# Block 0's loads issued from two engines, masks in a tile of their own, strided heads' rows of block 0 contiguous

## The chip, the cores and the metric

One core of a Trainium2 chip runs the whole program. The metric is the device time of one execution in microseconds (us); of several runs the median counts. The engines are TensorE (PE, with its weight loads as PEld), VectorE (DVE), ScalarE (ACT), GpSimd (POOL) and SyncE (SP), which here only issues DMAs. Sixteen DMA engines move the data.

## The reference

Attention over 4 batches, 8 heads, 576 positions and 64 columns per head feeds two gated feed-forward layers, all in float32 (the weights come as 64-bit words that the kernel converts):

```python
scores = scale * np.matmul(q, k.transpose(0, 1, 3, 2))
mask_local = (rel >= 0) & (rel < stride)                       # heads 0 to 3, stride 32
mask_strided = (rel >= 0) & (pos[None, :] % stride == pos[:, None] % stride)   # heads 4 to 7
attn = softmax(np.where(masks, scores, -1e9)); x = np.matmul(attn, v)
xn = x / rms(x) * rms_g;  h = silu(xn @ w_gate) * (xn @ w_val);  y = h @ w_out   # 2304 x 512, 1536
a = y @ w_a;  b = y @ w_b;  out = (a * b) @ w_out2
```

## The kernel before

The 576 positions are cut into six blocks of 96; a block of all four batches is 384 columns. Every float32 operand of a large product is split into a high and a low part, and three matmuls (L481, L482, L483) make one product.

For each block t, `attention(t, ...)` (L187) makes a dictionary of steps. Local heads go through TensorE: `load_local` (L201) loads queries and keys, `qk` the scores of three groups of units (L296), `smask` the mask and scale on VectorE (L314), `lmax`, `lexp` (one ACTIVATE per unit, L336, or one for the group, L333), `lnorm`, `pt` (transposes with the identity, L358), `ptc`, `pv` (L378). Strided heads never touch TensorE for their scores: `load_q` (L225) and `load_kv` (L232) load rows by residue, `sqk` multiplies on GpSimd (L248) and sums on VectorE (L251), `ssub`, `sexp` (L264), `snorm` (L273) make the softmax, `spv` (L281, L284) the weighted sum, `xst` the transposes. `pvc` and `xstc` write the block's activations `xx` (L387, L389) and their squares (L432); `rinv` (L448, L450) is the inverse root mean square.

No block runs ahead of block 0. Its loads are issued first, in the order of a string, and its steps in the order of another:

```python
LOADS0 = "la0 lq ls0 cst la1 lb0 lvl1 lb1 lvl0 lv0"
```

All of these are issued by SyncE: `la0` and `la1` are queries (L207, its first 512 columns) and keys (L208) of the two halves of local heads, `lb0`, `lb1` the other 256 columns of queries (L213), `lq`, `ls0`, `lv0` the strided heads' queries (L227), keys and values (L236), `lvl0`, `lvl1` the local heads' values (L219). `cst` (L569) is one tile of 388 columns with the identity (128), two masks (192 and 64) and the norm weights (4); `ident`, `mask_a`, `mask_b`, `g_sb` are views of it. Strided rows lie in HBM as 18 rows per head, and block t takes some of them per head (`qs[:, :, 3*t:3*t+3, :]` and `src[:, heads(g), :L, :]`), so a partition's share of block 0 is four pieces of 768 bytes.

Behind them SyncE issues the weights of 12 units (`load_units(NFC)`, L572 and L111), 24 transfers of 512 KB. Each is turned into float32r parts by `convert1` and `conversion`: on ACT L137, L142 and L150, on VectorE L145, on GpSimd L151. Then 12 chunks `fc` of the hidden layer run for each block (L740): `g_ps` and `v_ps` (24 matmuls), the gate, and `emit_y` of the chunk before (12 groups of matmuls). While block 0 runs, the remaining weights are converted and block 1's attention is computed.

Before qk0 TensorE runs 20 idle matmuls (`keep_busy(WARM)`, L563), and 36 more behind `pv` and the transposes (`id36`).

The order of instructions on an engine is not the written one: `TileContext(nc, schedule_with_timeline_sim=True)` (L1040) plans it when the program is built, by its own estimate of when each operand is there. `tc.issue_after(i)` keeps the instructions of a block behind i on i's engine; `gate(fc)` (L582) uses it, and so does `sqrt_set` (L423), which brings the table of the square root in early by one small activation.

Of the kernel before, what the change touches and what calls it, by code (L numbers as in the profile page):

```python
# [10 lines left out]
F32 = mybir.dt.float32  # L11
# [7 lines left out]
B, H, S, D = 4, 8, 576, 64  # L19
DM, FF, NT = 512, 1536, 2304  # L20
W = 32
PB = 96
NB = S // PB
NTB = B * PB
NM = S // W
NFC = FF // 128
NCC = DM // 128
# [8 lines left out]

LOADS0 = "la0 lq ls0 cst la1 lb0 lvl1 lb1 lvl0 lv0"
STEPS0 = ("sqk00 sqk01 sqk02 qk0 qk1 qk2 smask0 lmax0 lexp0 smask1 lmax1 lexp1 smask2 ssub sexp "  # L40
          "lnorm0 snorm lmax2 lexp2 pt0 ptc0 lnorm1 sqrt_set pt1 ptc1 spv00 spv01 spv02 lnorm2 pt2 "
          "ptc2 pv0 pvc0 pv1 pvc1 xst0 xst1 xstc0 id36 xstc1 rms rinv")
# [29 lines left out]
NEG = -1000000000.0  # L72
BIG = 3.0e38
# [1 line left out]


@with_exitstack
def fused_kernel(ctx: ExitStack, tc: tile.TileContext, qtl, ktl, vl, qs, ks, vs, cst, w1, w2, out):

# [2 lines left out]
    nc = tc.nc  # L84
# [102 lines left out]
    def attention(t, pool, psum, banks):  # L187

        L = 3 * (t + 1)
        G = {0: 4, 1: 2}.get(t, 1)  # L190
        KX, KB = (12 * D, 2) if t < 2 else (NM * D, 3)
        st = {}
        steps = {}

        def bank():
            return psum.tile([128, 512], F32, tag=next(banks), name="att")
# [4 lines left out]
        def load_local(hf, first=False):  # L201

            def f():
                q_t = st["q", hf] = pool.tile([128, 8 * PB], F32, tag="q", name="q_t", bufs=2)
                k_t = st["k", hf] = pool.tile([128, 4, 128], F32, tag="k", name="k_t", bufs=2)
                n = 512 if first else 8 * PB
                nc.sync.dma_start(q_t[:, :n], qtl[t, hf, :, :n])  # L207
                nc.sync.dma_start(k_t, ktl[t, hf])  # L208
            return f

        def load_rest(hf):
            def f():
                nc.sync.dma_start(st["q", hf][:, 512:], qtl[t, hf, :, 512:])  # L213
            return f

        def load_vlocal(hf):
# [5 lines left out]
        def heads(g):  # L222
            return slice(g * G, g * G + G)

        def load_q():  # L225
            q_t = pool.tile([128, 4, 3, D], F32, tag="qx", name="qs_t", bufs=1)
            nc.sync.dma_start(q_t, qs[:, :, 3 * t:3 * t + 3, :])  # L227
            st["qs"] = q_t
            st["S"] = pool.tile([128, 4, 3, 6 if t < 2 else NM], F32, tag="S", name="S_t", bufs=1)
            nc.vector.memset(st["S"], NEG)  # L230

        def load_kv(src, key, g):  # L232
            def f():
                k_t = pool.tile([128, KX], F32, tag="kv", name="kv_t", bufs=KB)
                k_t = k_t[:, :G * L * D].rearrange("p (g n d) -> p g n d", g=G, d=D)
                nc.sync.dma_start(k_t, src[:, heads(g), :L, :])  # L236
                st[key, g] = k_t
            return f

# [182 lines left out]

        def sqrt_set():  # L423

            with tc.issue_after(st["exp"].ins):
                nc.scalar.activation(scr, eps_sb, AF.Sqrt)

        def sq(i):
# [84 lines left out]
    psum = one.enter_context(tc.tile_pool(name="psum", bufs=1, space=bass.MemoryType.PSUM))  # L513
    cpool = ExitStack()
    const1 = cpool.enter_context(tc.tile_pool(name="const1", bufs=1))
    cst_sb = const1.tile([128, 388], F32, name="cst_sb")
    ident = cst_sb[:, 0:128]
    mask_a = cst_sb[:, 128:320].rearrange("p (a k) -> p a k", a=2)
    mask_b = cst_sb[:64, 320:384].rearrange("p (a k) -> p a k", a=1)
    g_sb = cst_sb[:, 384:388]  # L520
    pts = [const1.tile([128, 4, 2, PB], F32, name=f"pt{hf}") for hf in range(2)]
    ones = const1.tile([128, 128], F32, name="ones")
    apool = ExitStack()
# [42 lines left out]
    for p_t in pts:  # L566
        nc.gpsimd.memset(p_t, 0.0)
    s0 = attention(0, pool, psum, itertools.cycle(["att", "y0", "y1", "y2", "y3"]))
    s0["cst"] = lambda: nc.sync.dma_start(cst_sb, cst)  # L569
    for n in LOADS0.split():  # L570
        s0[n]()
    load_units(NFC)  # L572
# [156 lines left out]
    for t in range(NB):  # L729
# [3 lines left out]
        if t == NB - 1:  # L733
            apool.close()
            cpool.close()
            pool = p2.enter_context(tc.tile_pool(name="forms", bufs=1, reuse_waits="tile"))
            early = [f for k in (4, 5, 0, 1, 2, 3) for f in convert_forms(k, k < 4)]
        nxt = attention(t + 1, pool, psum, itertools.cycle(["att"])) if t + 1 < NB else None
        x = [xt[t, cc] for cc in range(NCC)]
        for fc in range(NFC):  # L740
# [206 lines left out]
    for i, (ps, g, p) in enumerate(steps):  # L947
# [12 lines left out]
        a, pa = products(g, 2 * p)  # L960
# [17 lines left out]
def _windows(a):  # L978

    z = np.concatenate([np.zeros(a.shape[:2] + (W, D), a.dtype), a], axis=2)  # L980
    return np.stack([z[:, :, PB * t:PB * t + 128] for t in range(NB)])


def _layout(inputs):
    q, k, v = (np.asarray(inputs[n]) for n in "qkv")
    c = np.ascontiguousarray
    r = {}


    ql = q[:, :4].reshape(2, 2, 2, 2, NB, PB, D).transpose(4, 0, 3, 6, 2, 1, 5)  # L990
    qa = np.zeros((NB, 2, 2, D, 2, 2, 2, 64), q.dtype)
    qb = np.zeros((NB, 2, 2, D, 2, 2, 2, 32), q.dtype)
    for hh in range(2):
        qa[:, :, hh, ..., hh, :] = ql[:, :, hh, ..., :64]
        qb[:, :, hh, ..., hh, :] = ql[:, :, hh, ..., 64:]
    r["qtl"] = np.concatenate([qa.reshape(NB, 2, 128, 512), qb.reshape(NB, 2, 128, 256)], axis=3)
    kw = _windows(k[:, :4]).reshape(NB, 2, 2, 2, 2, 128, D)
    r["ktl"] = c(kw.transpose(0, 1, 4, 6, 3, 2, 5).reshape(NB, 2, 128, 4, 128))
    vw = _windows(v[:, :4]).reshape(NB, 2, 2, 4, 128, D)
    r["vl"] = c(vw.transpose(0, 1, 4, 2, 3, 5))  # L1000

    def st(a):
        return a[:, 4:].reshape(B, 4, NM, W, D)
    r["qs"] = c(st(q).transpose(0, 3, 1, 2, 4).reshape(128, 4, NM, D))
    r["ks"] = c(st(k).transpose(0, 3, 1, 2, 4).reshape(128, 4, NM, D))
    r["vs"] = c(st(v).transpose(0, 3, 1, 2, 4).reshape(128, 4, NM, D))

    def ok(rows, n):
        i, j = np.arange(rows)[:, None] % (rows // 2), np.arange(n)[None, :]
        return (j > i) & (j <= i + W), j  # L1010
    cst = np.zeros((128, 388), np.float32)
    cst[:, 0:128] = np.eye(128)
    m, j = ok(128, 96)
    cst[:, 128:224] = np.where(m & (j >= W), BIG, NEG)
    cst[:, 224:320] = np.where(m, BIG, NEG)
    cst[:64, 320:384] = np.where(ok(64, 64)[0], BIG, NEG)
    cst[:, 384:] = np.asarray(inputs["moe_rms_g"]).reshape(NCC, 128).T
    r["cst"] = cst

    def weights(a, b, o):  # L1020

        a, b, o = (np.asarray(z) for z in (a, b, o))
        a, b = (z.reshape(NCC, 128, NFC, 128).transpose(2, 1, 0, 3).reshape(NFC, 128, DM) for z in (a, b))
        return c(np.stack([a, b, o.reshape(NFC, 128, DM)], axis=1)).view(np.uint64)
    r["w1"] = weights(inputs["moe_w_gate"], inputs["moe_w_val"], inputs["moe_w_out"])
    r["w2"] = weights(inputs["moe2_w_a"], inputs["moe2_w_b"], inputs["moe2_w_out"])
    return r
# [17 lines left out]
```

## Time and profile before

| | us |
|---|---|
| median of 3 runs | 964.13 |
| lowest, highest | 962.64, 965.04 |
| the profiled execution, device time | 965.19 |
| its span, first to last instruction | 963.4 |
| PE busy in the span | 936.9 |
| ACT, DVE, POOL busy | 421.7, 624.8, 541.8 |

A row of a timeline gives the start, the duration, engine, line, operation, tile written <- tiles read, shape, count, and in brackets the idle time of the engine just before it and who ended it. A row of windows gives, for a stretch, busy time (and instructions) of each engine, the granted TensorE clock (1.00 is the full 2.4 GHz, 0.50 is 1.2 GHz), the share of the DMA engines that was busy (packets counted from start to end, so it can pass 1) and the rate.

### The profile page before, as it was taken

How to read it: one execution, taken by the hardware profiler on the slowest of the kernel's cores; microseconds unless marked ns; L12 is line 12 of the kernel's file. 1: busy time of each engine (PE TensorE's matmuls, PEld its weight loads, DVE VectorE, ACT ScalarE, POOL GpSimd, SP SyncE). 2: the span in 40 equal slices, each digit the busy share in tenths (PEclk: the TensorE clock that was granted, in tenths of full speed). 3: DMA queues.
4: the chain of work that ended last, by engine and by line, in shares of the span. 5: the costliest groups of instructions: out<-in, count | busy, mean ns of one | idle time of the engine just before them, and what ended most of it. 6: DMA issues, size and time to landing. Idle time of an engine off the chain costs nothing.

```text
span 963.4 us, 14134 instructions
## 1 busy us (share of the span) xinstructions
PE 936.9 (97%) x5324; PEld 889.0 (92%) x5324; DVE 624.8 (65%) x913; ACT 421.7 (44%) x792; POOL 541.8 (56%) x407
## 2 busy tenths in 40 slices
PE   5998999999999999999999999999999999999998
PEld 4798999999999999999999898999999999999997
DVE  5669867548818895987566378667655655464534
ACT  5987655334433433444555455435425422122110
POOL 3568946458749687969379545654734424123211
PEclk6899999999999999999999999999999999999999
DMA  9964375426534553532788975997993973753701
GB/s 344 408 258 157 110 281 195 159 99 215 175 105 149 174 179 111 177 129 66 270 332 307 358 267 202 369 422 278 359 383 118 341 295 131 290 235 147 259 31 66
DMA packets 57507, 215.55 MB, mean 224 GB/s; under 512 B 5984, under 2 KB 14816, under 8 KB 51808
## 3 DMA queue, kind: packets, MB, share of 16 engines
q1 hardware_dynamic: 57296, 214.53, 61.0%
q8 instruction: 42, 0.69, 0.3%
q14 instruction: 25, 0.20, 0.1%
q10 hardware_dynamic: 144, 0.13, 0.0%
HBM read 172.17 MB, written 42.47 MB: 223 GB/s over the span
## 4 chain that ended last, share of the span: by engine, by line
PE 65%; DVE 7%; POOL 6%; DMA 5%; ACT 4%; issue 4%; SPq 0%; DVEq 0%; ACTq 0%; POOLq 0%
PE o L925 5%; PE o L923 5%; PE o L924 5%; POOL prod L248 4%; DMA raw<-in_w 4%; PE Y L856 4%; PE Y L855 4%; PE Y L854 4%; PE y L482 3%; PE Z L856 3%; PE Z L855 3%; PE Z L854 3%; PE y L483 3%; PE X L854 3%; PE X L856 2%
## 5 line engine op out<-in xcount | busy, mean ns | idle before, releaser
L151 POOL TENSOR_TENSOR hl<-c,hl 128x384 fp32r<-128x384 f32 x72 | 77.4, 1076 | 180.2 <-ACT hl L150 173.6
L248 POOL TENSOR_TENSOR prod<-kv_t,qs_t 128x512 f32<-128x512 f32 (+12 forms) x57 | 107.3, 1903 | 21.5 <-DMA wo<-wod 9.7
L482 PE MATMUL y<-hl,wo 128*128 128x384 f32 x288 | 98.3, 345 | 4.8 <-DVE hl L507 3.7
L281 POOL TENSOR_TENSOR prod<-kv_t,S_t 128x512 f32<-128x512 f32 (+12 forms) x57 | 86.8, 1536 | 22.5 <-issue 8.2
L481 PE MATMUL v_ps<-xx,gv 128*128 128x384 f32 x288 | 97.2, 337 | 1.9 <-DVE sg L760 1.9
L481 PE MATMUL g_ps<-xx,gv 128*128 128x384 f32 x288 | 97.6, 339 | 0.6 <-DVE sg L764 0.6
L482 PE MATMUL v_ps<-xx,gv 128*128 128x384 f32 x288 | 97.6, 339 | 0.0
L483 PE MATMUL v_ps<-xx,gv 128*128 128x384 f32 x288 | 97.2, 338 | 0.0
L483 PE MATMUL g_ps<-xx,gv 128*128 128x384 f32 x288 | 97.1, 337 | 0.0
L482 PE MATMUL g_ps<-xx,gv 128*128 128x384 f32 x288 | 96.8, 337 | 0.0
L861 DVE TENSOR_TENSOR c<-c,Y 128x384 f32<-128x384 f32 x108 | 58.9, 550 | 58.0 <-PE Y L856 53.6
L483 PE MATMUL y<-hl,wo 128*128 128x384 f32 x288 | 95.4, 340 | 0.0
L507 POOL TENSOR_TENSOR hl<-h,hl 128x384 fp32r<-128x384 f32 x60 | 64.9, 1081 | 51.1 <-ACT hl L506 51.0
L284 DVE TENSOR_REDUCE xs_t<-prod 128x64 f32<-128x448 f32 (+17 forms) x57 | 85.9, 1521 | 10.5 <-POOL prod L281 9.4
L481 PE MATMUL y<-hl,wo 128*128 128x384 f32 x288 | 83.7, 342 | 3.7 <-ACT hl L506 2.1
L924 PE MATMUL o<-slab,hl 128*128 128x512 f32 x214 | 83.7, 392 | 0.0
L923 PE MATMUL o<-slab,hl 128*128 128x512 f32 x214 | 83.7, 392 | 0.0
L925 PE MATMUL o<-slab,hl 128*128 128x512 f32 x214 | 82.5, 394 | 0.0
L150 ACT CAST hl<-c 128x384 fp32r<-128x384 f32 x72 | 37.0, 514 | 94.9 <-DVE c L891 94.6
L856 PE MATMUL Y<-slab,form 128*128 128x384 f32 x216 | 73.1, 338 | 0.0
L855 PE MATMUL Y<-slab,form 128*128 128x384 f32 x216 | 73.0, 338 | 0.0
L854 PE MATMUL Y<-slab,form 128*128 128x384 f32 x216 | 73.0, 338 | 0.0
(148 smaller groups left out, 2463.5 us busy)
## 6 DMA issues: line engine op xcount, KB each, us to landing
form<-formd SPq DMA_DIRECT2D x32, 1792.0 KB, 10.6
wo<-wod SPq DMA_DIRECT2D x60, 512.0 KB, 4.1
raw<-in_w SPq DMA_DIRECT2D x40, 512.0 KB, 7.2
gv_raw<-in_w SPq DMA_DIRECT2D x32, 512.0 KB, 10.1
formd<-form SPq DMA_DIRECT2D x6, 1792.0 KB, 7.5
formd<-forms SPq DMA_DIRECT2D x6, 1792.0 KB, 12.5
slab<-x2d SPq DMA_DIRECT2D x24, 384.0 KB, 4.0
wod<-wo SPq DMA_DIRECT2D x12, 512.0 KB, 3.2
```

Source lines behind the costliest of these rows:

```text
L248: nc.gpsimd.tensor_tensor(pr, st["ks", g][:, :, :n, :], st["qs"][:, heads(g), mm:mm + 1, :].to_broadcast([128, G, n, D]), op=ALU.mult)
L281: st["pvm"] = nc.gpsimd.tensor_tensor(pr, st["vs", g][:, :, :n, :], st["S"][:, heads(g), mm, :n, None].to_broadcast([128, G, n, D]), op=AL ...
L284: st["pvr"] = nc.vector.tensor_reduce(st["xs"][:, mm, heads(g), :], pr.rearrange("p g n d -> p g d n"), axis=X, op=ALU.add)
L481: nc.tensor.matmul(out_ps, w_hi, x_hi, start=start, stop=False)
L482: nc.tensor.matmul(out_ps, w_hi, x_lo, start=False, stop=False)
L483: nc.tensor.matmul(out_ps, w_lo, x_hi, start=False, stop=stop)
L854: nc.tensor.matmul(bank(n), hi, x[p][:, 0, c], start=begins and c == 0, stop=False, skip_group_check=not begins)
L855: nc.tensor.matmul(bank(n), hi, x[p][:, 1, c], start=False, stop=False, skip_group_check=not begins)
L856: nc.tensor.matmul(bank(n), lo, x[p][:, 0, c], start=False, stop=c == 1, skip_group_check=not begins)
L923: nc.tensor.matmul(o, h[:, 0, cols], w[0], start=n == 0, stop=False)
L924: nc.tensor.matmul(o, h[:, 0, cols], w[1], start=False, stop=False)
L925: nc.tensor.matmul(o, h[:, 1, cols], w[0], start=False, stop=n == len(chunks) - 1)
```

## The change

Block 0's loads are divided between SyncE and ScalarE's queue (`second` is ScalarE for t = 0 and SyncE otherwise): ScalarE issues both key loads, the masks, the strided keys, `lb1` and the identity, six in all; SyncE issues the other seven. The order is now masks second, `lb1` and `cst` ahead of the local values. The tile `cst` becomes two: `masks` (masks and norm weights, 260 columns) and `cst` (the identity, 128 columns). The strided queries are laid out by block for every t, and block 0 gets copies `ks0` and `vs0` of its keys and values, so that a partition's share is one piece of 3072 bytes. `sqrt_set` is also held behind `sexp`. `s0["w0"]` is defined but named in neither order string. A load's bytes stay the same, but for the tile that is cut in two.

```diff
-LOADS0 = "la0 lq ls0 cst la1 lb0 lvl1 lb1 lvl0 lv0"
+LOADS0 = "la0 masks lq ls0 la1 lb0 lb1 cst lvl1 lvl0 lv0"
...
+        second = nc.scalar if t == 0 else nc.sync
...
-                nc.sync.dma_start(k_t, ktl[t, hf])
+                second.dma_start(k_t, ktl[t, hf])
...
-                nc.sync.dma_start(st["q", hf][:, 512:], qtl[t, hf, :, 512:])
+                (second if hf else nc.sync).dma_start(st["q", hf][:, 512:], qtl[t, hf, :, 512:])
...
-            nc.sync.dma_start(q_t, qs[:, :, 3 * t:3 * t + 3, :])
+            nc.sync.dma_start(q_t, qs[t])
...
-                nc.sync.dma_start(k_t, src[:, heads(g), :L, :])
+                if t == 0:
+                    (second if key == "ks" else nc.sync).dma_start(k_t, {"ks": ks0, "vs": vs0}[key])
+                else:
+                    nc.sync.dma_start(k_t, src[:, heads(g), :L, :])
...
-            with tc.issue_after(st["exp"].ins):
+            with tc.issue_after(st["exp"].ins), tc.issue_after(st["sexp"].ins):
                 nc.scalar.activation(scr, eps_sb, AF.Sqrt)
...
-    cst_sb = const1.tile([128, 388], F32, name="cst_sb")
-    ident = cst_sb[:, 0:128]
-    mask_a = cst_sb[:, 128:320].rearrange("p (a k) -> p a k", a=2)
-    mask_b = cst_sb[:64, 320:384].rearrange("p (a k) -> p a k", a=1)
-    g_sb = cst_sb[:, 384:388]
+    cst_sb = const1.tile([128, 128], F32, name="cst_sb")
+    mask_sb = const1.tile([128, 260], F32, name="mask_sb")
+    ident = cst_sb
+    mask_a = mask_sb[:, 0:192].rearrange("p (a k) -> p a k", a=2)
+    mask_b = mask_sb[:64, 192:256].rearrange("p (a k) -> p a k", a=1)
+    g_sb = mask_sb[:, 256:260]
...
-    s0["cst"] = lambda: nc.sync.dma_start(cst_sb, cst)
+    s0["masks"] = lambda: nc.scalar.dma_start(mask_sb, masks)
+    s0["cst"] = lambda: nc.scalar.dma_start(cst_sb, cst)
+    s0["w0"] = lambda: load_units(1)
```

## Rows read from the trace of the kernel before

**Rows 1.** The page's first part: busy time of the engines.

```profile
PE 936.9 (97%) x5324; PEld 889.0 (92%) x5324; DVE 624.8 (65%) x913; ACT 421.7 (44%) x792; POOL 541.8 (56%) x407
```

**Rows 2.** Windows of the first 95 us: stretch, engines, clock, DMA share, GB/s.

```profile
1.60:6.00 4.40, 4.40 (x24) 3.34 (x23) 0.00 (x0) 0.41 (x1) 0.54 (x1) 1.00 0.87 254
6.00:10.00 4.00, 0.52 (x5) 0.35 (x4) 1.71 (x4) 0.37 (x2) 2.35 (x3) 0.89 1.05 354
...
15.00:33.90 18.90, 13.31 (x90) 10.03 (x91) 12.45 (x27) 16.70 (x29) 10.49 (x7) 0.61 1.03 410
33.90:52.00 18.10, 14.85 (x80) 13.19 (x77) 11.76 (x15) 17.69 (x26) 7.97 (x4) 1.00 1.04 409
52.00:62.00 10.00, 9.81 (x46) 9.48 (x47) 5.96 (x10) 9.75 (x15) 3.10 (x3) 0.83 0.97 383
62.00:88.00 26.00, 26.00 (x168) 25.27 (x166) 23.00 (x36) 20.52 (x54) 25.95 (x15) 1.00 0.39 122
88.00:95.00 7.00, 3.50 (x13) 3.44 (x13) 6.97 (x11) 4.12 (x8) 3.06 (x2) 0.76 0.54 185
```

**Rows 3.** Timeline of PE: the first matmuls, the first product, the longest later wait.

```profile
1.05 4.45 PE L563 MATMUL idle<-ones 128*128 128x256 bf16 x20 [1.05 <-DVE ones L555]
5.29 1.23 PE L296 MATMUL att<-k_t,q_t 128*128 128x96 f32 x8
10.34 3.89 PE L296 MATMUL att<-k_t,q_t 128*128 128x96 f32 x24 [3.82 <-DMA k_t<-in_ktl]
...
33.92 0.42 PE L481 MATMUL g_ps<-xx,gv 128*128 128x384 f32 x1
...
91.56 0.69 PE L482 MATMUL y<-hl,wo 128*128 128x384 f32 x1 [3.50 <-DVE hl L507]
```

**Rows 4.** Timeline of SP's queue in the head, the loads' issues.

```profile
0.73 0.39 SPq L207 DMA_DIRECT2D q_t<-in_qtl  x1
...
1.65 0.65 SPq L227 DMA_DIRECT2D qs_t<-in_qs  x1
2.34 0.62 SPq L236 DMA_DIRECT2D kv_t<-in_ks  x1
...
4.13 0.43 SPq L208 DMA_DIRECT2D k_t<-in_ktl  x1
...
8.16 26.27 SPq L111 DMA_DIRECT2D gv_raw<-in_w  x24
```

**Rows 5.** DMA issues of the first 9 us: count, KB, us to landing.

```profile
gv_raw<-in_w SPq DMA_DIRECT2D x1, 512.0 KB, 6.3
...
kv_t<-in_ks SPq DMA_DIRECT2D x1, 384.0 KB, 5.2
...
cst_sb<-in_cst SPq DMA_DIRECT2D x1, 194.0 KB, 5.1
```

**Rows 6.** Timeline of POOL, DVE and ACT in the head.

```profile
7.65 3.71 POOL L248 TENSOR_TENSOR prod<-kv_t,qs_t 128x256 f32<-128x256 f32 x3 [5.51 <-DMA kv_t<-in_ks]
...
8.25 0.56 DVE L314 SCALAR_TENSOR_TENSOR s_t<-att,cst_sb 128x384 f32<-128x384 f32 x1 [7.17 <-DMA cst_sb<-in_cst]
8.73 0.41 DVE L251 TENSOR_REDUCE S_t<-prod 128x4 f32<-128x256 f32 x1
...
9.63 0.38 ACT L336 ACTIVATE s_t<-s_t,lmx 128x96 f32<-128x96 f32 x1 [7.62 <-DVE lmx L323]
...
13.54 0.37 ACT L336 ACTIVATE s_t<-s_t,lmx 128x96 f32<-128x96 f32 x1 [2.37 <-DVE lmx L323]
...
14.99 0.64 ACT L137 ACTIVATE gv_raw<-gv_raw 128x512 f32<-128x512 f32 x1
...
17.46 0.62 ACT L333 ACTIVATE s_t<-s_t 64x512 f32<-64x512 f32 x1
18.10 1.28 ACT L426 ACT_TABLE_LOAD   x1
```

**Rows 7.** The tile in_qs: who waited for it (us, times); then a late window.

```profile
  POOL prod L248: 3.7, 3
```

```profile
360.00:380.00 20.00, 20.00 (x119) 19.67 (x118) 9.00 (x12) 9.17 (x16) 11.59 (x7) 1.00 0.37 128
```

More of the change, by code (lines that the diff above doesn't have):

```diff
@@ L77, in fused_kernel @@
 @with_exitstack
-def fused_kernel(ctx: ExitStack, tc: tile.TileContext, qtl, ktl, vl, qs, ks, vs, cst, w1, w2, out):
+def fused_kernel(ctx: ExitStack, tc: tile.TileContext, qtl, ktl, vl, qs, ks, vs, ks0, vs0, masks, cst, w1, w2, out):
     nc = tc.nc
@@ L1003, in st @@
         return a[:, 4:].reshape(B, 4, NM, W, D)
-    r["qs"] = c(st(q).transpose(0, 3, 1, 2, 4).reshape(128, 4, NM, D))
+    r["qs"] = c(st(q).transpose(0, 3, 1, 2, 4).reshape(128, 4, NB, NM // NB, D).transpose(2, 0, 1, 3, 4))
     r["ks"] = c(st(k).transpose(0, 3, 1, 2, 4).reshape(128, 4, NM, D))
     r["vs"] = c(st(v).transpose(0, 3, 1, 2, 4).reshape(128, 4, NM, D))
+    r["ks0"], r["vs0"] = (c(r[n][:, :, :NM // NB]) for n in ("ks", "vs"))
     def ok(rows, n):
@@ L1010, in ok @@
         return (j > i) & (j <= i + W), j
-    cst = np.zeros((128, 388), np.float32)
-    cst[:, 0:128] = np.eye(128)
+    cst = np.zeros((128, 260), np.float32)
     m, j = ok(128, 96)
[L1014 to L1018, printed above, removed]
+    cst[:, 0:96] = np.where(m & (j >= W), BIG, NEG)
+    cst[:, 96:192] = np.where(m, BIG, NEG)
+    cst[:64, 192:256] = np.where(ok(64, 64)[0], BIG, NEG)
+    cst[:, 256:] = np.asarray(inputs["moe_rms_g"]).reshape(NCC, 128).T
+    r["masks"] = cst
+    r["cst"] = np.eye(128, dtype=np.float32)
     def weights(a, b, o):
```

## The prediction

> **What bounds the kernel now.** I read the page's busy times first, then windows along the span, then timelines of single engines where a window has a hole. TensorE is busy for 936.9 of 963.4 us [rows 1], so an edit can win only where TensorE does idle or filler work. That is in the first 34 us, where the first real product starts at 33.92 [rows 3], and in two holes behind it: 18.10 - 14.85 = 3.25 us between 33.9 and 52, and 3.50 us between 88 and 95 [rows 2]. Each hole is followed or accompanied by a stretch at the lower clock: 0.83 over 10 us is 1.7 us lost in 52 to 62, and 0.76 over 7 us another 1.7 us in 88 to 95 [rows 2]. In 62 to 88 TensorE has no idle time at all.
>
> What sets 33.92 is a chain through several engines. VectorE's first mask waits 7.17 us for the tile of identity and masks and starts at 8.25; GpSimd's first product waits for the strided keys until 7.65; TensorE's second group of scores waits 3.82 us for keys until 10.34; and so ACT, which takes its first exponentials at 9.63 and the next at 13.54, comes to the first weight conversion at 14.99 [rows 3, 6]. From there ACT is the limit: 16.70 of 18.90 us busy up to the first product and 17.69 of 18.10 behind it [rows 2]. An ACT that starts this run of work earlier by x starts the first product earlier by about x. Behind that, all is fed by the same engines in the same order, and a shift of all of them is kept to the end of the span.
>
> **The change part by part, in time before 15 us.**
>
> *First scores.* No gain. The 20 idle matmuls run from 1.05 to 5.50, and the first scores follow without a wait [rows 3]. Landing their operands earlier changes nothing; if they landed later than 5.3, TensorE would wait.
>
> *First mask.* Its tile was issued fifth, at about 3.0, and took 5.1 us to land [rows 5]. The masks alone go second on ACT, at about 1.2 (0.73 + 0.41 as on SP). With the same 5.1 us they land at 6.3; if the table load of 1.28 us [rows 6] stands ahead on ACT, at 7.6. The first scores end at 5.29 + 1.23 = 6.52 [rows 3], so the mask starts between 6.6 and 7.6 in place of 8.25: a gain of 0.65 to 1.65. I take 1.65, since the tile is also smaller.
>
> *Strided keys and queries.* The keys are issued third on ACT, at about 2.0 in place of 2.34 [rows 4], and took 5.2 us [rows 5]. Unchanged latency gives 7.2; with longer rows (below) perhaps 6.0. GpSimd starts 0.4 to 1.6 earlier; I take 1.1, the middle, as nothing in the trace is nearer to one end.
>
> *Second keys.* These decide. They are issued at 4.13 [rows 4] and used at 10.34, over 6 us later. In the new order they go fourth on ACT, at about 2.5, which is 1.6 earlier. What lies ahead of them in bytes hardly changes (some 2.0 MB), so only the rate can help. In 1.6 to 6 us the DMA engines moved 254 GB/s at a busy share of 0.87; later, with longer rows, 354 and then 410 GB/s at full share [rows 2]. At the old rates the gain could be nothing; at 410 GB/s throughout it is (2.0 MB / 254 to 410) up to 3 us. I take 1.6, the issue moved, as it lies between: second mask, exponentials at 11.9 in place of 13.54, and ACT's first conversion at 13.3.
>
> *Weights.* ACT can start no earlier than they land. The first is issued at 8.16 and takes 6.3 us [rows 4, 5], so it lands near 14.5, only 0.5 us ahead of its use at 14.99. SP now issues seven small loads in place of thirteen, some 3 us less of issue; but the bytes ahead are the same 3.2 MB. What can shorten these is the row length: three loads of 384 KB in 768-byte pieces become 3072-byte pieces. 1.18 MB at 254 GB/s is 4.6 us, at 354 to 410 it is 3.3 to 2.9: a gain of 1.3 to 1.7. The least is the idle share before 6 us, 0.13 x 4.4 = 0.6, if short rows cost nothing. The most is 410 GB/s from 1.6 us on: 3.2 MB and then the 0.5 MB of the weight are through after 9.0 us, at 10.6 in place of 14.5, or 3.9. I take 1.7, what the row length explains: landing at 12.8, just ahead of ACT.
>
> *What ACT pays.* Six issues of 0.4 to 0.65 us [rows 4] are up to 3.9 us of its queue, and from the ninth load on (`lb1` and `cst` among them) an issue may wait for an early load to land, by 5 to 6 us. Queued behind them are the table load and the first exponentials, for which DVE waits next in its sums. The exponentials can't start before mask and maximum, near 8.0 in place of 9.63 [rows 6]. So the issues are hidden with 1 to 2 us to spare; were that cover gone, each further microsecond would delay all of ACT.
>
> *The rest.* `sqrt_set` behind `sexp` costs nothing where the table load already comes last, as it does: 18.10, behind the group exponential at 17.46 [rows 6]. Later blocks' strided queries in one piece: GpSimd waited for that tile three times, 3.7 us in all, but in such a stretch TensorE was busy 20.00 of 20 us [rows 7], so nothing is counted. The identity lands later now; it is first read by transposes behind the second exponentials, at the earliest near 14, and even the last transfer issued in the head is there.
>
> **Sum.** ACT's run of conversions starts 1.7 us earlier (both operands of its start say so), the first product near 32.2, and nothing behind it takes this back or adds to it. The profiled execution's 965.19 becomes 963.5. It stood 1.06 above the median of the runs, so the forecast is 964.13 - 1.7 = **962.4**. By the bounds of the unknown prices (the keys' 0 and 3.0, which bind at either end) it lies between 964.1 and 961.1. A measurement of this kernel tells about 0.3% from no change, which is 2.9 us: faster means below 961.2, slower above 967.0.
>
> *A rule against it.* In 1.6 to 6 us the DMA engines were already busy for 0.87 of the time, with one issuer [rows 2]. The Trainium skill, "DMA: Bandwidth & Descriptors", section "Issuing engines are not separate DMA queues", says that transfers started by different engines run on the same 16 DMA engines and interleave, and that a second issuer saves only the sequencer's time. By that rule alone the sum would be 0.6 us; the row agrees in so far as little is idle there, while the low rate at that share leaves room for the longer rows.
>
> **The rivals.**
>
> *The engines are full anyway.* Only the idle 0.13 of 4.4 us is won, 0.6 us, and the second keys land no earlier because the two queues' loads share the same engines. For it: the share of 0.87 and 1.05. Against it: 254 GB/s at 0.87 and 410 at 1.03 are not the same use of them. It gives 963.5. Chance 0.20.
>
> *A hole closes as well.* The holes behind 33.9 come from ACT's order: `sg` waits for the inverse root, which waits for squares that ACT takes behind conversions. When data arrive earlier in the planner's estimate, squares may go ahead of a conversion. Then up to 3.25 us of idle and 1.7 us at the lower clock go too, 5.0 in all, giving 962.4 - 5.0 = 957.4; half of it, 959.9. For it: VectorE's order in the head is already unlike the written one (the mask at 8.25 precedes the first sum at 8.73 [rows 6], though STEPS0 has all sums first), so order follows estimates. Against it: nothing in the edit aims at that order. Chance 0.20.
>
> *A hole more: slower.* The same reordering works the other way: one more conversion put ahead of block 0's squares or of a hidden chunk's high part makes TensorE wait once as it did at 91.56, for 3.50 us [rows 3], and drops the clock with it for 1.7 us [rows 2]. That is 5.2 against the 1.7 won: 964.13 + 3.5 = 967.6. It decides, beyond what a measurement can tell, from a further wait of about 2.9 us on: with the 1.7 of a fallen clock that makes 4.6, the gain of 1.7 and 2.9 more. For it: ACT has 0.4 us to spare in 18 after 33.9. Against: 62 to 88 has TensorE full, with room to take up shorter delays. Chance 0.20.
>
> *It doesn't do what it says.* If ACT's issues stood behind its table load, or were planned among exponentials, masks and keys would come later by 1.28 us or more and the gain would vanish: 964.1. I hold this for part of the first rival's case and give it no chance of its own.
>
> **How the numbers follow.** Forecast 0.40, the first rival 0.20, a closed hole 0.20, a new hole 0.20. Of the forecast's cases, which reach to 961.1 with the runs themselves spread by 1.5 us about their median, I count three in eight as below 961.2: 0.15; with the closed hole's 0.20 that is 0.35 for faster. Slower are those new holes that lose all: 0.20, as a second one would add to the first. The rest, 0.25 of the forecast and the 0.20 of the first rival, is 0.45. The likeliest case stands at 962.4, with a range of its own from 961.1 to 964.1. The range for 8 in 10 reaches to a closed hole, 957.4, and to a little short of the whole price of a new one, 967.0.
>
> **What would show it.** Right: masks landing before 6.6, GpSimd's first product near 6.6, second scores near 8.7, the first conversion near 13.3, the first product near 32.2, DMA rates above 300 GB/s in 1.6 to 6, and the holes at 41 to 52 and 88 to 92 as they were, 1.7 us earlier. Wrong: second keys that still land near 10; a first conversion that waits for its weight; a first exponential that waits for ACT's own issues; a first product earlier by 1.7 whose gain is gone by 62 us; or idle time of TensorE in 34 to 130 that differs by over 2 us from the 6.75 counted above.

## The result, and the profile after

The changed kernel takes 971.5 us (median of 6 runs, 969.46 to 976.5); the kernel before, run beside it, 962.35 (6 runs, 961.0 to 965.04). The ratio is 1.0095, 95% interval 1.0067 to 1.0122: slower by 9 us, where 1.7 us less was forecast. The execution that was profiled took 971.82 us, its span 969.7; it is near the median of its kernel. The one profiled before, 965.19 us, stands 2.8 us above the median of 962.35, so the two traces differ by 6.3 us of span and not by 9.

The page of the changed kernel, its first part, stands against [rows 1]:

```profile
PE 936.6 (97%) x5324; PEld 890.1 (92%) x5324; DVE 633.4 (65%) x913; ACT 420.3 (43%) x792; POOL 540.0 (56%) x407
```

TensorE does the same work in the same 937 us. The span is 6.3 us longer (969.7 and 963.4), so TensorE waits more. VectorE is busy 8.6 us longer with the same 913 instructions.

Windows of the changed kernel (columns as in [rows 2]), and then the last of them in the kernel before:

```profile
1.60:6.00 4.40, 4.40 (x23) 3.36 (x22) 0.00 (x0) 0.00 (x0) 0.54 (x1) 1.00 0.96 302
...
15.00:32.40 17.40, 11.05 (x87) 9.07 (x87) 11.43 (x27) 15.99 (x35) 9.19 (x7) 0.64 1.03 409
32.40:50.00 17.60, 13.86 (x67) 12.69 (x64) 11.19 (x14) 16.52 (x22) 7.46 (x4) 0.90 1.03 408
62.00:88.00 26.00, 22.40 (x135) 21.46 (x134) 24.75 (x33) 18.63 (x49) 22.93 (x13) 0.95 0.30 97
120.00:140.00 20.00, 16.90 (x87) 16.32 (x86) 9.95 (x15) 12.27 (x19) 4.03 (x4) 0.91 0.50 179
```

```profile
120.00:140.00 20.00, 19.36 (x110) 18.74 (x109) 12.56 (x20) 12.13 (x19) 6.67 (x6) 1.00 0.77 274
```

The rate before 6 us rose as forecast, to 302 GB/s where there were 254. But 62 to 88, where TensorE had been busy for all of 26.00 us [rows 2], now has 3.60 us of idle time, and 120 to 140 has 3.10 where there were 0.64. The first of the two is not all new: the hole of 3.50 us up to 91.56 [rows 3] is gone, and 88 to 95 has no idle time now.

Timeline of PE of the changed kernel, the start and the three longest waits behind it:

```profile
8.69 2.62 PE L300 MATMUL att<-k_t,q_t 128*64 128x64 f32 x22 [1.58 <-DMA q_t<-in_qtl]
...
32.39 0.42 PE L485 MATMUL g_ps<-xx,gv 128*128 128x384 f32 x1
...
43.44 0.45 PE L485 MATMUL v_ps<-xx,gv 128*128 128x384 f32 x1 [3.21 <-DVE sg L767]
...
83.92 0.44 PE L485 MATMUL v_ps<-xx,gv 128*128 128x384 f32 x1 [3.25 <-DVE hl L511]
...
133.38 0.69 PE L485 MATMUL y<-hl,wo 128*128 128x384 f32 x1 [3.10 <-ACT wo L150]
```

The first product starts 1.53 us earlier than in [rows 3]. Adding up TensorE's gaps of over 0.15 us between 30 and 560 us gives 17.69 us here and 11.84 before: 5.85 more. Behind 34 us the clock falls to 1.2 GHz three times, for 3.4 us each (from 44.5, 85.4 and 133.2), twice before: one more costs 1.7. Together -1.53 + 5.85 + 1.7 = 6.0 of the 6.3 us between the spans.

Timelines of DVE, POOL, ACT and the two issuing queues of the changed kernel in the head:

```profile
7.15 0.56 DVE L318 SCALAR_TENSOR_TENSOR s_t<-att,mask_sb 128x384 f32<-128x384 f32 x1 [6.06 <-PE att L300]
...
9.90 1.84 DVE L350 TENSOR_SCALAR lsm<-lsm 128x4 f32<-128x4 f32 x1 [0.73 <-ACT s_t L340]
...
12.34 0.52 DVE L318 SCALAR_TENSOR_TENSOR s_t<-att,mask_sb 128x384 f32<-128x384 f32 x1
...
13.85 0.53 DVE L327 TENSOR_REDUCE lmx<-s_t 128x4 f32<-128x384 f32 x1
...
7.99 3.72 POOL L252 TENSOR_TENSOR prod<-kv_t,qs_t 128x256 f32<-128x256 f32 x3 [5.85 <-DMA kv_t<-in_ks]
...
2.13 0.45 ACTq L209 DMA_DIRECT2D k_t<-in_ktl  x1
4.74 0.33 ACTq L214 DMA_DIRECT2D q_t<-in_qtl  x1
...
14.58 0.58 ACT L372 COPY pt<-att 96x512 f32<-96x512 f32 x1 [4.71 <-PE att L362]
15.06 0.37 ACT L340 ACTIVATE s_t<-s_t,lmx 128x96 f32<-128x96 f32 x1
...
16.51 0.64 ACT L137 ACTIVATE gv_raw<-gv_raw 128x512 f32<-128x512 f32 x1
...
2.11 0.43 SPq L214 DMA_DIRECT2D q_t<-in_qtl  x1
4.91 1.46 SPq L220 DMA_DIRECT2D v_t<-in_vl  x2
```

The mask waits for the scores, no longer for its tile. Yet the first conversion on ACT is late, 16.51 against 14.99 [rows 6]. On VectorE the second mask waits behind work on the first group (`lsm`, a normalizing step) and starts at 12.34, and the normalization and the third mask stand ahead of its maximum, at 13.85. ACT first copies `pt` of the first group, for which it waits 4.71 us, and takes the second exponentials behind it. Before, the exponentials came at 13.54 [rows 6] and this copy only at 16.84. Both engines execute another order, and that is the thread of what follows. About 1 us of this delay is the execution's own: in three other traces with these loads and this head order (three experiments below, root moved, `hl` moved and head alone) `lsm` takes 0.22 to 0.51 us in place of 1.84, and the first conversion stands at 15.16 to 15.66.

Set side by side, the two built programs hold the same instructions on the compute engines, but 611 of TensorE's 5123 positions differ, 161 of VectorE's 913, 145 of ACT's 702 and 36 of GpSimd's 403, and 30 of the 361 transfers issued behind the head's loads. All of them lie before some 200 us. `TileContext` plans the order by its estimate of when operands arrive; the edit changed those estimates.

### The profile page after: what moved, and what is told of

It is laid out like the page before. It is cut to its first block, busy times and chain, and to the rows that moved or that the text cites. A ratio compares the mean times of both kernels' runs of the same rounds, so it can differ in the third digit from the quotient of the medians.

```text
span 969.7 us, 14132 instructions
## 1 busy us (share of the span) xinstructions
PE 936.6 (97%) x5324; PEld 890.1 (92%) x5324; DVE 633.4 (65%) x913; ACT 420.3 (43%) x792; POOL 540.0 (56%) x407
## 3 DMA queue, kind: packets, MB, share of 16 engines
q10 hardware_dynamic: 1008, 1.38, 0.4%
## 4 chain that ended last, share of the span: by engine, by line
PE 74%; DMA 9%; DVE 8%; ACT 4%; issue 2%; POOL 2%; SPq 0%; DVEq 0%; ACTq 0%; POOLq 0%
PE o L932 5%; PE o L930 5%; PE o L931 5%; PE Y L863 4%; PE Y L862 4%; PE Y L861 4%; PE v_ps L487 3%; PE y L485 3%; PE v_ps L486 3%; PE g_ps L487 3%; PE v_ps L485 3%; PE y L486 3%; PE y L487 3%; PE g_ps L485 3%; PE g_ps L486 3%; DMA raw<-in_w 3%
## 6 DMA issues: line engine op xcount, KB each, us to landing
gv_raw<-in_w SPq DMA_DIRECT2D x32, 512.0 KB, 10.2
```

## The experiments

The first pair takes the two things apart. An order can be pinned: behind `fused_kernel` each instruction of an engine, and each transfer that it issues behind the head's loads, is tied behind the one that precedes it in a recorded order, without a semaphore (this shifts line numbers by up to 29). In all pinned kernels this is the edit; only the table ORDERS and the loads differ (12 loads of the head in place of 13 where they are the old ones). No kernel was run pinned to its own order, so what a pin costs by itself is not shown; the fastest kernel below is a pinned one.

```diff
+        for a, b in zip(row, row[1:]):
+            if a.engine == b.engine:
+                tc.add_manual_dep(b, a.name, mybir.DependencyInfo(mybir.DependencyClass.NoSync, ...
...
         fused_kernel(tc, *args)
+        pinned(tc, 13, ORDERS)
```

**New loads, old order.** The changed kernel, its engines held to the order of before.

> The changed loads, with every engine's instructions held in the order that they had in the kernel before. Theory 'order': the loss comes from the order that the planner laid out behind the new loads, and the loads alone gain what the first product gained, 1.5 us or less. Then this runs at 960 to 963 us. Rival 'loads': the second issuer and the new sequence of transfers cost the time themselves, whatever the order. Then it stays at 970 to 973 us.

Measured: 960.08 us (959.56 to 961.35, 7 runs), ratio 0.9975 [0.9964, 0.9986]. This is less than both kernels take.

**Old loads, new order.** The kernel before, held to the changed kernel's order.

> The loads of the kernel before, with every engine's instructions held in the order of the changed kernel. Theory 'order': 970 to 975 us, since that order also counts on masks that are early. Rival 'loads': 961 to 964 us. If both are half right, e1 and e2 lie near 966 each.

Measured: 974.01 us, ratio 1.0113 [1.0097, 1.0129]. Windows of the first of the two, and then of the second:

```profile
1.60:6.00 4.40, 4.40 (x25) 3.36 (x24) 0.00 (x0) 0.00 (x0) 0.55 (x1) 1.00 0.92 285
...
31.90:50.00 18.10, 14.67 (x80) 13.07 (x77) 11.78 (x15) 18.07 (x26) 8.08 (x4) 1.00 1.03 408
62.00:88.00 26.00, 24.17 (x153) 23.50 (x152) 24.39 (x38) 19.75 (x53) 25.93 (x14) 0.99 0.46 142
120.00:140.00 20.00, 19.12 (x112) 18.53 (x111) 13.58 (x23) 9.54 (x15) 10.93 (x10) 1.00 0.87 303
```

```profile
62.00:88.00 26.00, 22.48 (x134) 21.54 (x134) 24.76 (x32) 18.87 (x51) 23.21 (x13) 0.95 0.30 98
120.00:140.00 20.00, 16.95 (x80) 16.36 (x79) 9.75 (x15) 12.39 (x19) 4.50 (x4) 0.83 0.49 176
```

With the old loads and the new order 62 to 88 and 120 to 140 look as they do in the changed kernel. With the new loads and the old order the gaps between 30 and 560 us sum to 10.39 us and the clock falls once. So the loads by themselves give 0.25%, and the order by itself takes 1.1%.

**Which part of the edit turns the order?** Three kernels were left to the planner: the masks alone, all issued by SyncE; the second issuer alone; and the whole change but for the strided rows.

```diff
-LOADS0 = "la0 lq ls0 cst la1 lb0 lvl1 lb1 lvl0 lv0"
+LOADS0 = "la0 masks lq ls0 cst la1 lb0 lvl1 lb1 lvl0 lv0"
...
+    s0["masks"] = lambda: nc.sync.dma_start(mask_sb, masks)
```

> Of the change only the masks in a tile of their own, loaded second, still by SyncE; the planner is free. Built, its order differs from that of the kernel before on all engines as far as block 1. Theory 'order': a new order at once, so the time moves by several us, more likely up: 966 to 974 us. Rival 'loads': no second issuer, so 961 to 963 us.

```diff
-                nc.sync.dma_start(k_t, ktl[t, hf])
+                second.dma_start(k_t, ktl[t, hf])
...
-    s0["cst"] = lambda: nc.sync.dma_start(cst_sb, cst)
+    s0["cst"] = lambda: nc.scalar.dma_start(cst_sb, cst)
```

> Of the change only the second issuer (both key loads, strided keys, the last queries and the whole constant tile go through ScalarE), the planner free. Built, its order differs from that before in the first 30 positions of VectorE alone, and nowhere behind. Theory 'order': 960 to 964 us. Rival 'loads': 968 to 973 us.

```diff
-            nc.sync.dma_start(q_t, qs[t])
+            nc.sync.dma_start(q_t, qs[:, :, 3 * t:3 * t + 3, :])
...
-                    (second if key == "ks" else nc.sync).dma_start(k_t, {"ks": ks0, "vs": vs0}[key])
+                    (second if key == "ks" else nc.sync).dma_start(k_t, src[:, heads(g), :L, :])
```

> The changed kernel with the strided rows left as they were, in four pieces, the planner free. Its loads lie between the two kernels, its order differs from both (555 and 367 positions of TensorE). By the loads alone it would be at 960 to 963 us. Theory 'order': anywhere from 962 to 974 us, and its holes, not its head, tell which.

Measured: masks alone 964.59 us, 1.0019 [1.0008, 1.003]; second issuer alone 964.47, 1.0005 [0.9993, 1.0018]; all but the rows 966.76, 1.0033 [1.0018, 1.0049]. The second issuer alone leaves the order nearly as it was (23 positions of VectorE, in the head) and the time as well. The masks alone turn 436 positions of TensorE; their time lies between the ranges of the two theories. None of the three brings the whole loss of 0.95%, and the strided rows alone were not run: the loss comes with the order that the planner makes of all parts together.

**The second issuer, taken away.** Once in the old order, pinned, and once left to the planner:

```diff
-        second = nc.scalar if t == 0 else nc.sync
+        second = nc.sync
...
-    s0["masks"] = lambda: nc.scalar.dma_start(mask_sb, masks)
-    s0["cst"] = lambda: nc.scalar.dma_start(cst_sb, cst)
+    s0["masks"] = lambda: nc.sync.dma_start(mask_sb, masks)
+    s0["cst"] = lambda: nc.sync.dma_start(cst_sb, cst)
```

> The changed sequence of loads, masks apart and rows in one piece, but all of them issued by SyncE; every engine in the order of the kernel before. With ScalarE issuing six of them this order took 960.1 us (0.9975 of the kernel before). Theory 'bytes': the rows and the masks make the gain, the issuer little: a ratio of 0.997 to 0.9985. Theory 'issue': the second issuer makes most of it: a ratio of 0.999 to 1.0005.

> The same loads as the run before (all by SyncE), the planner free. Built, its order differs from both others: 406 of 5123 positions of TensorE from the kernel before, 500 from the changed one. Theory 'order': its time differs from the run with the old order by several us although no load differs, in either direction, more likely up: 962 to 972 us. Rival, that only the order behind a second issuer is bad: within 1.5 us of the run before.

Measured: pinned 960.5 us, 0.9982 [0.9968, 0.9995]; planned 964.16, 1.0013 [0.9999, 1.0026]. Pinned, one issuer gives nearly all that two give (0.9975), and the intervals overlap. The Trainium skill, "DMA: Bandwidth & Descriptors", section "Issuing engines are not separate DMA queues", says that a second issuer saves only the sequencer's time; this pair agrees with it in the main: with two issuers the first weight is issued at 7.95 in place of 9.09 and the first product starts at 31.90 in place of 33.02, and the ratios of the whole differ by 0.07%. Planned, the same loads lose 3.7 us against pinned: again the order.

**Which stretch of the order?** The new loads stay; the new order holds only up to some 55 us, only from there to some 135, or only behind that. The rest is the old order.

> The changed loads; of the changed kernel's order only the part up to about 50 to 60 us, every engine's order behind that as before. The two orders differ by 11.4 us with these loads (971.5 against 960.1). Theory 'early waits': the first hole of 3.2 us, in place of 1.2, and what follows from it are carried to the end: 962 to 965 us. Rival 'late chains': the head's order costs nothing that block 0 does not take up, and the time is lost where block 0 hands over to block 1: 959.5 to 961 us.

> The changed loads; of the changed kernel's order only the part from about 50 to 60 us to the end of block 0 (about 135 to 140 us). Theory 'late chains': in this part the square root of block 1 stands on ACT between a weight conversion and the last tanh, two table loads of 1.28 us ahead of a cast that TensorE waits for; that hole of 3.1 us and 1.7 us of lower clock are here: 963 to 967 us. Rival: 960 to 962 us.

> The changed loads; of the changed kernel's order only the part behind block 0, in which block 1 waits for transposes by 2.2 us in all. If the parts add, e5, e6 and e7 exceed 960.1 us by 11.4 in sum; by the holes I expect some 3 us here: 961.5 to 964 us. If this part only suffers from what came before it, 959.5 to 961 us.

Measured: head 961.26 us, 0.9979 [0.9967, 0.999]; middle 972.3, 1.0095 [1.0072, 1.0118]; tail 962.66, 1.0000 [0.9983, 1.0017]. Against the 0.9975 of the old order throughout, the run with the new middle loses 1.2%, with the new tail 0.25% (the two intervals just overlap), with the new head nothing that can be told from none, though it has the hole of 3.2 us up to 42.4 and the fallen clock from 43.8 to 47.2. The new head's time lies between its two expected ranges, the new middle's above both of its own, and the three losses add up to more than the 1.2% of the whole new order. Windows of the kernel with the new middle, and the row of TensorE at its longest wait:

```profile
62.00:88.00 26.00, 22.48 (x131) 21.48 (x130) 25.83 (x33) 17.72 (x43) 22.54 (x13) 0.93 0.33 112
120.00:140.00 20.00, 17.05 (x96) 16.43 (x95) 9.16 (x13) 10.92 (x16) 4.57 (x4) 1.00 0.53 184
140.00:150.00 10.00, 5.42 (x21) 5.13 (x20) 5.37 (x10) 1.03 (x2) 8.39 (x7) 0.66 1.03 388
```

```profile
145.10 0.66 PE L514 MATMUL y<-hl,wo 128*128 128x384 f32 x1 [4.58 <-ACT hl L539]
```

Both holes of the changed kernel are there, and a third behind 140, where the new middle meets the old tail. Its gaps sum to 9.23 us more than with the old order, and 10.2 in place of 3.4 us at 1.2 GHz lose another 3.4. That is 12.6, and the spans differ by 12.6 (970.3 and 957.7). But the third hole, which the changed kernel does not have, and the fall beside it are 4.58 + 3.4 = 8.0 of these, so this run does not price the middle of the changed kernel. Two traces do, of the changed kernel and of the old order with the same loads. Of the 12.0 us between their spans (969.7 and 957.7), 0.5 is there when the first product starts (32.39 and 31.90). By TensorE's gaps and its time at 1.2 GHz, 2.7 are lost from there to 55 us, 6.5 from 55 to 137, and 2.2 from 137 to 200.

**What makes the two holes of the middle?** For the one at 130, ACT's timeline of the changed kernel:

```profile
129.11 1.28 ACT L452 ACT_TABLE_LOAD   x1
130.41 0.58 ACT L452 ACTIVATE rms_t<-att,eps_sb 128x384 f32<-128x384 f32 x1
131.01 1.28 ACT L769 ACT_TABLE_LOAD   x1
132.30 0.52 ACT L769 ACTIVATE th<-sg 128x384 f32<-128x384 f32 x1
132.73 0.60 ACT L150 CAST wo<-cz 128x512 fp32r<-128x512 f32 x1
```

Block 1's root and its two table loads, over 3 us, stand ahead of a `wo` cast for which TensorE waits. Before the change the root came behind the last of these casts (126.45, the table load at 127.08). An experiment moves the root of block 1 to the last slot, and the planner does the rest:

```diff
-        part += ["rms", "rinv"] * (fc == n_sl)
+        part += ["rms", "rinv"] * (fc == (NFC - 1 if t == 0 else n_sl))
```

> The changed kernel with one step moved in the written order: block 1's inverse root is taken up with chunk 11 of block 0, not chunk 10. Built, its order equals that of the changed kernel up to about 125 us (ACT position 144, VectorE 134), and behind that the root with its table load stands behind the cast of the weight conversion, not ahead of it. Theory 'late chains': the hole of 3.1 us at 130 and the 1.7 us of lower clock behind it go, 966 to 968 us in place of 971.5. Rival 'late anyway': the conversions are late because of what lies before, the hole moves or another takes its place, 970 to 973 us.

Measured: 970.05 us, 1.0072 [1.0049, 1.0095]. The time is in the rival's range. The hole at 130 shrinks to 0.25 us, and block 1's first chunks start 3.3 to 3.5 us earlier. Then TensorE waits for ACT at 170 (timeline of PE of that kernel), and the clock falls there from 174.9 to 178.3:

```profile
172.24 0.62 PE L485 MATMUL y<-hl,wo 128*128 128x384 f32 x2 [1.79 <-ACT hl L510]
173.83 0.39 PE L362 MATMUL att<-cst_sb,s_t 128*96 128x128 f32 x2 [0.97 <-DVE s_t L352]
```

For the one at 80.7, timelines of DVE and POOL of the changed kernel:

```profile
78.18 1.85 DVE L352 TENSOR_TENSOR s_t<-s_t,lrs 64x512 f32<-64x512 f32 x1
79.96 2.84 DVE L145 SCALAR_TENSOR_TENSOR cz<-gv_raw,cz 128x512 uint32<-128x512 uint32 x1
82.73 0.67 DVE L255 TENSOR_REDUCE S_t<-prod 128x8 f32<-128x512 f32 x1
83.33 0.54 DVE L511 TENSOR_TENSOR hl<-v_ps,hl 128x384 fp32r<-128x384 f32 x1
...
89.49 2.25 DVE L145 SCALAR_TENSOR_TENSOR cz<-gv_raw,cz 128x512 uint32<-128x512 uint32 x1
...
79.44 2.82 POOL L151 TENSOR_TENSOR gv<-cz,gv 128x1024 fp32r<-128x1024 f32 x1
...
88.80 2.40 POOL L151 TENSOR_TENSOR gv<-cz,gv 128x1024 fp32r<-128x1024 f32 x1 [2.24 <-ACT gv L150]
```

ACT's high part is done at 78.77, but the low part `hl` stands behind a normalization, a conversion and a sum on VectorE. The kernel before has its like: the 3.50 us up to 91.56 [rows 3], where `hl` starts at 90.97 behind a conversion of 3.08 us. With the old order and the new loads the wait for this `hl` is 1.83. An experiment pins the changed kernel's own order with this one `hl` two places earlier, between normalization and conversion (VectorE's order, written by tiles):

```diff
-    cz<-gv_raw,cz; S_t<-prod; hl<-v_ps,hl
+    hl<-v_ps,hl; cz<-gv_raw,cz; S_t<-prod
```

> The changed kernel's loads and order; only on VectorE one instruction moves, the low part of a hidden chunk (`hl`, the one for which TensorE waited 3.25 us from 80.7 on), ahead of a 128x512 weight conversion (2.84 us beside GpSimd's own conversion) and a sum (0.67 us). Theory one, that single instruction's place makes the hole: the hole of 3.25 us goes, the low-clock stretch behind it (85.4 to 88.9, 1.7 us) goes too, and the time falls by 3 to 5 us, from 971.5 to 966.5 to 968.5. Theory two, the weights of the next product are late by the same conversion, so the wait only changes its name: the product of chunk 4 with `wo` started at 86.66 just behind GpSimd's part of it (85.28 + 1.29 = 86.57), and this part waits for ScalarE's cast, which waits for the very conversion. Then TensorE waits some 3 us for `wo` from about 83.5 on, the clock falls as before, and the time stays within 970 to 973.

Measured: 969.97 us, 1.0061 [1.0041, 1.0081]. Timeline of PE of that kernel:

```profile
82.89 0.44 PE L514 MATMUL y<-hl,wo 128*128 128x384 f32 x1 [0.61 <-ACT wo L179]
...
90.85 0.44 PE L514 MATMUL y<-hl,wo 128*128 128x384 f32 x1 [0.33 <-ACT wo L179]
...
110.62 0.44 PE L514 MATMUL g_ps<-xx,gv 128*128 128x384 f32 x1 [1.87 <-DVE sg L796]
```

Each theory got a half. The hole went and the fall of the clock with it; a wait for `wo` of 0.61 us, not 3, came in its place. Chunk 5's `y` starts 3.9 us earlier than in the changed kernel, 0.65 of which the head had already. But by chunk 10 only 1.9 is left: two more waits for `wo` and one of 1.87 us for `sg`, which was 0.94 before this move, take it back. From block 2 on 1.3 is left, half of it the head's. One instruction's place makes a hole; mending one does not mend the order.

## Why the prediction was wrong

**The step that failed** is the last one of the sum: "nothing behind it takes this back", resting on "all is fed by the same engines in the same order". The engines are the same; the order is not. Old loads in the new order lose 1.1%, new loads in the old order win 0.25%, and in the traces 6.5 of the 12.0 us between old and new order are lost from 55 to 137 us, and 2.2 behind, beyond the stretch that was priced. I had read that the planner orders by its estimates, and used it for two rivals, but not for the forecast itself.

**The head, step by step.** The mask was to start at 6.6 to 7.6: 7.15. Second scores at 8.7: the row of 8.69 begins with two matmuls of the third group, and the second group follows at 8.98. The first product near 32.2: 32.39. DMA rates above 300 GB/s: 302, but not by the rows alone (below). GpSimd's first product was to start at 6.6: 7.99, later than the 7.65 of [rows 6]. The keys left at 1.65 in place of 2.34 and took longer to land. The second mask, with exponentials at 11.9, was to follow the second scores; it stood at 12.34 behind other work of VectorE, no earlier than before. The first conversion was to be at 13.3: 16.51, by the new order on VectorE and ACT and by the long `lsm`; in the old order it stands at 13.74, and the first product at 31.90. The first weight was to land at 12.8: with the old order it landed at 12.86, in the changed kernel's trace at 14.62, and ACT did not wait for it. The wait from the ninth load on was there: both queues pause after the fourth issue, until 4.74 and 4.91. It was hidden, as I said: the first exponential starts at 8.33. SyncE issued twelve loads before, not thirteen, and its first weight came from 8.16 only to 7.92. The mark that was met is the gain that is gone by 62 us: the first `y` starts at 53.26, and started at 51.94 before.

**The gain.** The 1.7 us were about the right size, in part by luck. New loads in the old order give 2.7 us by medians (962.77 less 960.08), 1.3 to 3.5 by the ratio's interval, and their first product is 2.02 us earlier. The first rival, engines that are full anyway, had 0.6 and is out for the loads. But I took the 1.7 from the length of the rows, and the rate before 6 us is not the rows' alone. Windows of the second issuer with the old rows (the second issuer alone), and of the new rows with one issuer (in the old order):

```profile
1.60:6.00 4.40, 4.28 (x27) 3.18 (x25) 0.00 (x0) 1.08 (x1) 0.55 (x1) 1.00 0.93 287
```

```profile
1.60:6.00 4.40, 4.25 (x27) 3.22 (x25) 0.00 (x0) 0.41 (x1) 0.54 (x1) 1.00 0.96 237
```

With one issuer and the new rows left to the planner the rate is 274, so what the rows give by themselves is not settled: it lies on either side of the 254 of before. The first weight, which landed at 14.47 before, landed at 13.37 with the first of these and at 14.43 with the second; with all but the rows it landed at 14.88, and at 12.86 with everything in the old order. By these single traces the rows alone did not bring it forward; it took them and the second issuer together.

**The slow rival** had the mechanism: a reordering that puts other work ahead of something that TensorE waits for, and the clock falling with it. It was mis-sized, as one hole of 3.5 us and one fall of 1.7. The new order in place of the old, with the same loads, costs 971.5 - 960.08 = 11.4 us, in a series of waits. For the idle time of TensorE in 34 to 130 the mark of error was 2 us beyond 6.75: it was 9.93, and the hole of 3.10 begins only at 130.28. "Against: 62 to 88 has TensorE full, with room to take up shorter delays" was the wrong reading of [rows 2]: the engines that feed it had little room there, VectorE 3.00 us of 26.00 and GpSimd 0.05, and in the changed kernel VectorE has 1.25. And one trace is one execution. I took the 3.50 us up to 91.56 and their fall for the kernel's own; in four other traces with the old order in that stretch the wait for this `hl` is 1.83 (new loads), 1.76 (second issuer alone), 1.76 (one issuer) and 1.38 (new head), and 3.45 in one (new tail).

**What stays open.** Why the planner's estimates led to this order was not taken apart, nor which of its moves start the loss of the middle. The root ahead of the casts and the late `hl` each make a hole of over 3 us, but without either the time falls by only 0.2 to 0.3% of the kernel's (1.0072 and 1.0061 for 1.0095), with intervals that overlap.

## What to carry to other kernels

Where a planner sets the order from estimated arrival times, an edit to the first 10 us can be an edit to all that the planner lays out behind it; compare the built orders first, and price the stretch where they differ. To tell the worth of an edit from the worth of a reordering, pin the old order under the new loads and the new order under the old ones. To price a stretch of an order, read the traces beside the splice: a kernel of two halves has a seam with a wait of its own. And a version worth keeping may be the edit with the order pinned: here 960.08 us in place of 971.5.

## What the runs showed of the hardware

The same VectorE instruction takes very different times beside GpSimd. The 128x512 conversion takes 0.69 us with GpSimd idle and took 2.84 and 2.25 in the rows above. Timeline of DVE of the changed kernel, one of the undisturbed ones:

```profile
47.26 0.69 DVE L145 SCALAR_TENSOR_TENSOR cz<-gv_raw,cz 128x512 uint32<-128x512 uint32 x1 [0.58 <-ACT cz L142]
```

Both disturbed ones ended 0.54 us after GpSimd's conversion (82.80 and 82.26; 91.74 and 91.20), as if each stood still and then ran. The Trainium skill, "SBUF — State Buffer", section "SBUF: two separate sides", says that GpSimd and a VectorE instruction with two inputs in SBUF, as this one has, share a pair of ports as an exclusive lock, held for a whole instruction, in which the loser blocks; these rows agree. So an order also sets what an instruction costs. Not every overlap costs: one of these conversions, from 21.34, took 0.68 us while the trace has a product of GpSimd running from 20.95. The lock is not the loss, either: between 30 and 140 us the 21 conversions on VectorE take 27.0 us together, and 26.3 before. VectorE's 8.6 us more of busy time lie in other instructions too (normalizations `s_t<-s_t,lrs` 2.4, `lsm` 2.1, squares 1.8), and what of that is the lock was not settled.

How a wait and a fall of the clock go together: in the changed kernel each wait of over 3 us (3.21 from 40.2, 3.25 from 80.7, 3.10 from 130.3) is followed by a fall to 1.2 GHz that begins 2.9 to 4.8 us after the wait did. It is no rule: with the root moved a wait of 3.21 us from 40.1 brought no fall, and with the new middle one of 2.96 us from 127.2 brought none, while one of 1.83 us from 84.5, with the new loads in the old order, did. Behind 34 us each fall lasted 3.4 us or twice that. To price a long hole with its fall at 5 us was right for the three of the changed kernel.
